# Setup of a fused attention and convolution kernel: the first loads, the second chunk of x, GpSimd's order and VectorE's first factors are placed anew

## The chip, the core and the metric

The kernel runs on one core of a Trainium2 chip. The core has five engines that run side by side: TensorE (PE in the profile, and PEld for its weight loads), VectorE (DVE), ScalarE (ACT), GpSimd (POOL) and SyncE (SP). SP, ACT and POOL can each issue DMAs, and every engine works through its own instructions in the order in which they were written for it. The metric is the time of one execution on the device in microseconds (us), lower is better.

## The reference

Two independent parts, whose outputs are joined along the last axis. Part A is a long convolution of 576 channels over 2048 positions, whose kernel is built from 128 complex exponentials a channel. Part B is attention with 32 query heads of 18 numbers and one shared key and value head.

```
# A: u (1, 2048, 576); A, B, C (576, 128) complex
dt = exp(log_dt)[:, None]
P  = exp((dt * A)[:, :, None] * arange(2048))        # (576, 128, 2048)
K  = einsum("dn,dnl,dn->dl", C, P, dt * B).real      # the convolution's kernel
y  = causal_convolution(u, K) + u * Dskip            # by FFT of length 4096
# B: x (1, 2048, 576), 32 heads, Dh = 18
q = heads(x @ wq);  k = x @ wk;  v = x @ wv          # one k and v for all heads
p = softmax(einsum("bhqd,bkd->bhqk", q, k) * Dh ** -0.5)
b = merge_heads(einsum("bhqk,bkd->bhqd", p, v)) @ wo
out = concatenate([y, b], axis=-1)
```

## The kernel before, in words

**Attention** (class `Attention`) goes over the 2048 queries in four chunks of 512 columns (x0 to x3), in each over 8 groups of four heads, and in each group over 16 blocks of 128 keys. One score tile `s` is 128 keys by two heads by 512 queries: two matmuls (L543), each of the keys `kaug` against one head's queries `aug`. ScalarE turns it into `P` with one exponential (L552 in the first group, L554 later). `product` (L841) multiplies `P` with the values `v_sb` and adds into `ops` (L849). Three score tiles are in flight (`NS = 3`), so the main loop takes three at a time; such a set of three is called a round below. At the end of a group VectorE copies `ops` to `o` (`gather`, L561), and the next group's `ops` can start only then.

The queries of a chunk come from five projections `q` (L437), which VectorE splits in two f16 halves `qh` and `ql`; GpSimd's queue writes them to a DRAM buffer `qd` (L487), and SP's queue fetches each pair of heads back as `aug` (L532). A row `sh` that belongs to every head, a bound on its scores, goes the same way (L523).

**Convolution** (class `Conv`) goes over 12 chunks of 48 channels. `front` makes the kernel of a chunk: `powers` (L1112; ScalarE's Exp and Sin and VectorE's products), `factors` (L1190), `tables` (`tab`, L1256) on VectorE and `kgen` (`kg`, L1287) on TensorE. `back` transforms, multiplies and transforms back (`hu`, `lu`, `hk`, `lk`, `iy` on TensorE, long products on VectorE). These are generators: `Stream.advance` runs one to its next `yield`, and `conv.begin(n)` (L1466) runs the first one n steps, so that its instructions stand at that place in each engine's order.

**What sets the order.** In the main loop a planner (`fill`, L810) keeps a clock `K` with modelled costs (`K.t` for TensorE, `K.v` for VectorE, `K.a` for ScalarE) and puts pieces of the convolution and of the projections between the rounds of scores. All instructions of PE, ACT and DVE stand in source order (L1527); those of POOL are placed by the compiler's scheduler.

**The setup** (`setup`, L234, and the first four rounds of `main`) is where the change lies. It loads `wq[0]` on ScalarE's queue and x0, `wkv` and x1 on SP's; `conv.early()` (L1458) loads the first inputs of the convolution, `dt`, `ab`, `pos` and `raw`, on GpSimd's queue. Then come, in source order:

1. four warm-up products on zeros (`warm`), and `conv.begin(6)`: `powers` to the first Sin;
2. the projection `first` of x0 into keys of chunk 0 and queries of heads 0 to 4 and more (20 matmuls), whose f16 halves `h1` (ScalarE, L292) and `l1` (VectorE, L294) are the first `keys`. Eighteen-row DMAs copy them into `kaug` (L301) and into the first two `aug` (L305), on all three queues;
3. the loads of x2 and x3 on SP's queue (L324, `x_us`, `x_ks` and `x_acc`), and `conv.begin(4)`: the second Sin and the Exp of `powers`;
4. the projection `second` (keys of chunk 1, values of chunks 0 and 1, and queries; 20 matmuls, from x0 and x1), with the bound on the first group's scores between (`small`, `aw_first`, `bias`);
5. `main`: the first round of scores; `keys_1` (L376) splits `second` into halves (`h2`, `l2`), copies them to `kaug` (L355, SP and POOL) and transposes values (`va`); the second round; `keys_23` (L384) projects `third` from x2 and x3 in two pieces around the third round, splits it and copies it to `kaug` in twelve DMAs of SP; `settle` (L396) ends the keys (`vb`, `kmx`, `kmax`) and starts the loads of the other weights and of the convolution's `dft`. After that the planner works.

In the listing `x` is a tile of x0 or x1, and `keys` is the tile that holds all the halves.

## Time and profile before

| | us |
|---|---|
| median of three runs | 1170.29 |
| the three runs | 1166.37 to 1170.54 |
| the profiled execution, its own time | 1168.69 |
| the span of its trace | 1166.9 |
| TensorE busy | 1089.1 |
| VectorE busy | 999.0 |
| ScalarE busy | 998.9 |
| GpSimd busy | 142.1 |

The span runs from the first to the last instruction, 1.8 us less than the execution's own time. Times below count from the span's start. A row of the timeline has start, duration, engine, line, operation, output and inputs, and in brackets how long the engine sat idle before it and what ended that. A row of the chain has start, duration and what the end of the program waited for at that time. A row of the windows has, for each engine, busy time and the number of instructions, and then the granted TensorE clock (PEclk, 1.00 is full), the DMA engines' share and GB/s.

### The profile page before, as it was taken

The page shows a single profiled execution, that of the slowest core. Times are in us where ns is not written, and L with a number is a line of the kernel's source. Part 1 is how long each engine was busy: PE and PEld are TensorE (multiplying, and loading weights), DVE is VectorE, ACT ScalarE, POOL GpSimd, SP SyncE. Part 2 cuts the span into 40 slices and gives each one's busy share as a digit, 9 for nine tenths or more (in the row PEclk, how much of TensorE's full clock was granted, in tenths as well). Part 3 has the DMA queues.
Part 4 walks back from the last instruction along what each step waited for, and adds up shares of the span by engine and source line. Part 5 has one row for each costly group of instructions (what it writes and reads, how often), then busy time and mean ns, then how long its engine had stood idle before and what let it go on. Part 6 is the DMA issues. An engine that isn't in the chain of part 4 may idle for free.

```text
span 1166.9 us, 33114 instructions
## 1 busy us (share of the span) xinstructions
PE 1089.1 (93%) x13898; PEld 393.7 (34%) x13898; DVE 999.0 (86%) x1755; ACT 998.9 (86%) x1052; POOL 142.1 (12%) x258
## 2 busy tenths in 40 slices
PE   7889989999999999899999999989989999999997
PEld 2223333333333333324333333334322333433323
DVE  3668998899899898898899799898798899799693
ACT  4668998889888998998888889888999989899992
POOL 5131221122022000000221100001050000000000
PEclk9899999999999999999999999999999999999999
DMA  7421241213212202022222301202122200311201
GB/s 231 135 57 54 82 159 41 81 33 95 82 58 80 85 28 73 20 87 87 90 77 74 104 22 55 74 28 77 60 83 75 88 29 29 104 47 34 70 29 58
DMA packets 57595, 83.90 MB, mean 72 GB/s; under 512 B 13829, under 2 KB 33867, under 8 KB 56928
## 3 DMA queue, kind: packets, MB, share of 16 engines
q1 hardware_dynamic: 46191, 73.71, 19.1%
q0 software_dynamic: 11024, 7.63, 2.7%
q8 instruction: 111, 1.82, 0.6%
q10 hardware_dynamic: 225, 0.38, 0.1%
q14 instruction: 44, 0.36, 0.1%
HBM read 47.12 MB, written 33.85 MB: 69 GB/s over the span
## 4 chain that ended last, share of the span: by engine, by line
PE 58%; DVE 20%; ACT 11%; issue 6%; DMA 2%; POOL 1%; DVEq 0%; ACTq 0%; SPq 0%; POOLq 0%
PE ops L849 24%; PE s L543 15%; ACT P L554 11%; PE op L194 5%; PE q L437 4%; DVE tab L120 3%; PE iy L194 3%; DVE ks L120 3%; PE kg L1298 3%; DVE acc L120 2%; DVE t L120 2%; PE hu L194 1%; PE hk L194 1%; DVE fr L120 1%; PE fin L194 1%
## 5 line engine op out<-in xcount | busy, mean ns | idle before, releaser
L554 ACT ACTIVATE P<-s 128x1024 f32<-128x1024 f32 x992 | 934.5, 1034 | 119.6 <-PE s L543 117.4
L849 PE MATMUL ops<-P,v_sb 128*32 128x512 f32 x4096 | 510.5, 599 | 10.7 <-DVE o L124 10.4
L543 PE MATMUL s<-aug,kaug 55*128 55x512 f16 x2048 | 308.4, 381 | 42.6 <-ACT P L554 34.8
L543 PEld LDWEIGHTS <-kaug 55*128 55x128 f16 x2048 | 90.6, 94 | 378.0 <-issue 328.8
L849 PEld LDWEIGHTS ops<-P,v_sb 128*32 128x32 f32 x4096 | 117.2, 110 | 168.2 <-issue 127.5
L487 POOL DMA_DIRECT2D qd<-qh x116 | 65.7, 573 | 307.3 <-DVE qh L128 306.9
L437 PE MATMUL q<-x,wq_sb 128*32 128x256 f32 x1360 | 85.2, 386 | 0.2 <-DVE un L136 0.2
L194 PE MATMUL op<-wo_sb,oT 126*32 126x288 f32 (+1 forms) x1080 | 77.2, 410 | 2.6 <-DVE ob L124 1.4
L120 DVE TENSOR_TENSOR tab<-tab,tt 128x576 f32<-128x576 f32 (+1 forms) x72 | 59.1, 820 | 1.4
L124 DVE COPY ksb<-kg 128x192 f32<-128x192 f32 x48 | 17.4, 363 | 49.9 <-PE kg L1298 49.6
L120 DVE TENSOR_TENSOR tab<-tab 128x576 f32<-128x576 f32 (+1 forms) x72 | 58.7, 815 | 0.0
L120 DVE TENSOR_TENSOR tab<-fr,dif 128x576 f32<-128x576 f32 (+1 forms) x72 | 58.7, 815 | 0.0
L120 DVE TENSOR_TENSOR tab<-sum,fr 128x576 f32<-128x576 f32 (+1 forms) x72 | 58.7, 815 | 0.0
L120 DVE TENSOR_TENSOR tt<-fr,sum 128x576 f32<-128x576 f32 (+1 forms) x72 | 58.7, 815 | 0.0
L437 PEld LDWEIGHTS q<-x,wq_sb 128*32 128x32 f32 x1360 | 39.5, 110 | 39.8 <-issue 15.4
L1207 POOL MEMSET fr<- 128x192 f32 x24 | 12.9, 623 | 307.0 <-DVE tt L120 194.6
L120 DVE TENSOR_TENSOR acc<-acc,pt 128x1728 f32<-128x1728 f32 (+2 forms) x36 | 48.6, 1350 | 0.1
L120 DVE TENSOR_TENSOR pt<-us,ks 128x1728 f32<-128x1728 f32 (+2 forms) x36 | 48.3, 1349 | 0.1
L552 ACT ACTIVATE P<-s,bias 128x1024 f32<-128x1024 f32 x32 | 33.2, 1115 | 14.0 <-PE s L543 13.6
L194 PEld LDWEIGHTS op<-wo_sb,oT 126*32 126x32 f32 (+1 forms) x1080 | 30.3, 109 | 43.4 <-issue 17.5
L1298 PEld LDWEIGHTS kg<-tab 128*32 128x32 f32 x2304 | 35.7, 110 | 22.7 <-issue 7.9
L1298 PE MATMUL kg<-tab 128*32 128x64 f32 x2304 | 41.8, 220 | 1.2 <-DVE tab L120 0.8
(177 smaller groups left out, 1023.6 us busy)
## 6 DMA issues: line engine op xcount, KB each, us to landing
od<-o SPq DMA_DIRECT2D x31, 256.0 KB
aug<-qd SPq DMA_DIRECT2D x124, 55.0 KB
u<-u SPq DMA_DIRECT2D x12, 384.0 KB
kd<-ksb SPq DMA_DIRECT2D x12, 384.0 KB
kt<-kd SPq DMA_DIRECT2D x48, 96.0 KB
outa<-u SPq DMA_DIRECT2D x12, 384.0 KB
pw<-pw SPq DMA_DIRECT2D x8, 528.0 KB
oT<-od SPq DMA_DIRECT2D x16, 252.0 KB
```

Of the source, the lines that this page charges most:

```text
L120: return self.v.tensor_tensor(out, *a, **k)
L124: return self.v.tensor_copy(out, *a, **k)
L194: nc.tensor.matmul(ps[j:e], w[:, j:e], x, start=start, stop=stop, tile_position=(0, j))
L437: nc.tensor.matmul(ps[o, 256 * f:256 * f + 256], w[:, k, i], xt[:, k, x], start=(k == 0), stop=(k == 4), tile_position=(0, 32 * j))
L487: q.dma_start(qd[h:h + n, row + d:row + d + nd, cs], src[i1:i1 + n * nd, :cs.stop - cs.start])
L543: nc.tensor.matmul(ps[:, j, :], self.kaug[r, kb * P:(kb + 1) * P], t[r, :], start=True, stop=True)
L552: nc.scalar.activation(pt, ps, AF.Exp, bias=self.bias, scale=SCALE / QQ)
L554: nc.scalar.activation(pt, ps, AF.Exp, scale=SCALE / QQ)
L849: nc.tensor.matmul(o_ps[32 * j:32 * j + 32, :], self.v[:, kb, :], pts[exp(n, j // 2)][:, j % 2, :], start=(kb == 0), stop=(kb == 15), tile ...
L1207: nc.gpsimd.memset(t[:, :, 0:NF:8], one)
L1298: nc.tensor.matmul(ps[32 * g:32 * g + 32, d, :], t[:, :32], t[:, 32:], start=(j == 0), stop=(j == 1), tile_position=(0, 32 * g))
```

## The change

Five things are altered in the setup, and one follows from them.

- The convolution's first `dt`, `ab` and `pos` are issued on ScalarE's queue, behind `wq[0]`, and no longer on GpSimd's. `raw` stays on GpSimd's.
- x1 is loaded after `conv.begin(6)`. A memset by VectorE on a corner of x1 stands ahead of each of its two loads, so SP issues them when VectorE has come to that place.
- Three products on zeros (12 matmuls into `spare`, half a bank of `small`) stand where three fifths of `second` stood. One fifth comes ahead of the bound, one behind it, and the other three after the first round of scores. The bound ends earlier in TensorE's order.
- VectorE makes the first factors inside the setup: `conv.begin(3)` ahead of the first scores, `conv.begin(2)` behind `keys_1` and `conv.begin(1)` ahead of the second piece of `keys_23`. The transposes `va` move behind the second round. The planner's clock gets 3.5 in place of 1.5 there.
- POOL joins the engines in source order.
- The planner starts from another state, so all later pieces are placed anew.

```diff
--- before.py
+++ after.py
@@ -261,8 +261,6 @@
         nc.sync.dma_start(wkv, a["wkv"])
         nc.sync.dma_start(x0[:, 1:3, :], a["xT"][0, :, 1:3, :])
         nc.sync.dma_start(x0[:, 3:5, :], a["xT"][0, :, 3:5, :])
-        nc.sync.dma_start(x1[:, 0:3, :], a["xT"][1, :, 0:3, :])
-        nc.sync.dma_start(x1[:, 3:5, :], a["xT"][1, :, 3:5, :])
         conv.early()
         nc.gpsimd.dma_start(spread[:, 0:140], a["sel"][:, 45:185])
         nc.gpsimd.dma_start(self.sel, a["sel"][:, 0:45])
@@ -284,7 +282,11 @@
         self.todo, self.busy, self.group = [], False, 0
         self.side_work = Stream(self.side(), self.k, 99.0)
         conv.begin(6)
-        p1, small = (self.ps_s.tile([P, 2, CT], F32, tag="s", name=n)[:, 0, :] for n in ("first", "small"))
+        for k0, k1 in ((0, 3), (3, 5)):
+            V.memset(x1[0:1, k0:k1, 0:1], 0.0)
+            nc.sync.dma_start(x1[:, k0:k1, :], a["xT"][1, :, k0:k1, :])
+        p1, small = (self.ps_s.tile([P, 2, CT], F32, tag="s", name=n) for n in ("first", "small"))
+        p1, small, spare = p1[:, 0, :], small[:, 0, :], small[:, 1, 0:256]
         for k in range(5):
             for j in range(3):
                 self.project(p1, j, self.wq[0], 32 * j, 0, k)
@@ -324,17 +326,18 @@
                 nc.sync.dma_start(t[:, :, c - 2, :], a["xT"][c, :, k0:k1, :])
         conv.begin(4)
         self.pa = pa = self.bank(CT, "second")
-        for k in range(3):
-            self.second(k)
+        for _ in range(3):
+            matmul4(nc, spare, self.wo[:, 0, 0:P], self.wo[:, 0, P:P + 256])
         nc.tensor.matmul(small[:, 0:1], spread[:, 0:128], self.km[:, 0:1], start=True, stop=True)
         V.tensor_copy(self.kmax[:, 0:1], small[:, 0:1])
         aw = self.p2.tile([P, P], F32, tag="aw", name="aw_first")
         V.tensor_scalar(aw, ab[:, 0:1].broadcast_to([P, P]), self.kmax[:, 0:1], 1.002, op0=ALU.mult, op1=ALU.mult)
-        for k in range(3, 5):
-            self.second(k)
+        self.second(0)
         matmul4(nc, small[:, 8:12], aw, self.sel[:, 0:4])
         V.tensor_reduce(self.bias, small[:, 8:12], axis=AX.X, op=ALU.max)
         V.tensor_scalar(self.bias, self.bias, -SCALE / QQ, None, op0=ALU.mult)
+        self.second(1)
+        conv.begin(3)
 
     def project(self, ps, j, w, i, c, k):
         self.nc.tensor.matmul(ps[32 * j:32 * j + 32, :], w[:, k, i:i + 32], self.slice(c, k),
@@ -375,14 +378,16 @@
 
     def keys_1(self):
         nc, V = self.nc, self.V
+        for k in range(2, 5):
+            self.second(k)
         h2, l2 = self.parts[2:]
         self.halves(self.pa, h2, l2, 5)
         self.place(1, h2, l2, 0, (nc.sync, nc.gpsimd))
         self.largest(h2, 5)
-        self.values(self.ps_o.tile([P, CT], F32, tag="o", name="va"), 0, slice(1, 3))
 
     def keys_23(self, ks):
         if ks[0] == 0:
+            self.values(self.ps_o.tile([P, CT], F32, tag="o", name="va"), 0, slice(1, 3))
             self.pb = self.bank(CT, "third")
         for k in ks:
             self.third(k)
@@ -880,13 +885,15 @@
             s = self.step
             if r == 0:
                 self.keys_1()
-                K.t += 1.5
+                conv.begin(2)
+                K.t += 3.5
                 continue
             if r == NS:
                 self.keys_23((0, 1))
                 K.t += 2.1
                 continue
             if r == 2 * NS:
+                conv.begin(1)
                 self.keys_23((2, 3, 4))
                 K.t += 2.7
                 continue
@@ -1070,7 +1077,7 @@
         cs = slice(k0 * ND, k1 * ND)
         dt, ab = (self.pf.tile([P, n, 4 * ND], F32, tag=t, name=f"{t}{g}") for n, t in ((1, "dt"), (2, "ab")))
         n = (k1 - k0) * ND
-        q = nc.sync if g else nc.gpsimd
+        q = nc.sync if g else nc.scalar
         q.dma_start(dt[:, 0, :n], self.a["ldt"][cs].partition_broadcast(P))
         q.dma_start(ab[:, :, :n], self.a["pa"][:, :, cs])
         self.next_burst = dt[:, 0, :n], ab[:, :, :n]
@@ -1458,7 +1465,7 @@
     def early(self):
         nc = self.nc
         self.load_burst(0)
-        nc.gpsimd.dma_start(self.pos, self.a["pos"])
+        nc.scalar.dma_start(self.pos, self.a["pos"])
         self.load(0)
         self.n, self.burst = -1, False
         self.streams = [Stream(self.front(0), self.k)]
@@ -1524,7 +1531,7 @@
         at = Attention(tc, ctx, aps, clock)
         cv = Conv(tc, ctx, at.bank, aps, clock)
         cv.at, at.conv = at, cv
-        with tc.manual_schedule(engines={mybir.EngineType.PE, mybir.EngineType.Activation, mybir.EngineType.DVE}):
+        with tc.manual_schedule(engines={mybir.EngineType.PE, mybir.EngineType.Activation, mybir.EngineType.DVE, mybir.EngineType.Pool}):
             cv.setup()
             cv.open(ctx)
             at.open(ctx)
```

At the start, on ScalarE, these are the rows before and after (`dt`, `ab`, `pos` are the convolution's inputs, `pw` its powers, `keys` the halves of the projections):

```order
L259 DMA wq_sb<-wq 128x640
L1135 ACT_TABLE_LOAD
L1135 ACTIVATE dt_139<-dt_139 128x48
L1155 ACT_TABLE_LOAD
L1155 ACTIVATE pw_171<-pw_171 128x528
L292 ACTIVATE keys<-first 128x512
```

```order
L259 DMA wq_sb<-wq 128x640
L1081 DMA dt_137<-ldt 128x48
L1082 DMA ab_138<-pa 128x2x48
L1468 DMA pos_sb<-pos 128x22
L1142 ACT_TABLE_LOAD
L1142 ACTIVATE dt_137<-dt_137 128x48
L1162 ACT_TABLE_LOAD
L1162 ACTIVATE pw_169<-pw_169 128x528
L294 ACTIVATE keys<-first 128x512
```

Three loads moved in ahead of ScalarE's first table load; the Sin of `pw` stands ahead of the halves `keys` in both.

On SP after the change, with the semaphores on which each issue waits (x_126 is x1; DMAHW0 to 7 are eight semaphores that the DMAs of SP and ACT take in turn, each waiting for the one that had it before):

```order
L287 DMA x_126<-xT 128x1536 [waits DMAHW0_49,DVE_49]
L287 DMA x_126<-xT 128x1024 [waits DMAHW1_49,DVE_49]
L303 DMA kaug<-keys 18x512 [waits DMAHW5_49,Activation_49]
L303 DMA kaug<-keys 18x512 [waits DMAHW6_49]
L303 DMA kaug<-keys 18x512 [waits DMAHW7_49,DVE_49]
L303 DMA kaug<-keys 18x512 [waits DMAHW0_49]
L307 DMA aug_114<-keys 18x512 [waits DMAHW1_49]
L307 DMA aug_114<-keys 18x512 [waits DMAHW2_49]
```

The fourth copy to `kaug` now takes DMAHW0 after the first part of x1, and the first copy to `aug_114` takes DMAHW1 after the second part. Before, x1's loads stood ahead of all VectorE work, as the fifth and sixth load of SP.

On VectorE between the bound and the projection of x2 and x3, before (`bias` is the bound, `m` and `pw` are the powers' parts, `fr` and `t` the factors):

```order
L136 TENSOR_REDUCE bias_121<-small 128x1
L128 TENSOR_SCALAR bias_121<-bias_121 128x1
L128 TENSOR_SCALAR keys<-second 128x512
L132 SCALAR_TENSOR_TENSOR keys<-second,keys 128x512
L124 COPY keys<-second 128x512
L136 TENSOR_REDUCE km<-keys 128x1
L128 TENSOR_SCALAR km<-km 128x1
L124 COPY v_sb<-va 128x8x18
L128 TENSOR_SCALAR keys<-third 128x512
```

and after, from the bound to the halves of `second`:

```order
L128 TENSOR_SCALAR bias_121<-bias_121 128x1
L120 TENSOR_TENSOR pw_169<-pw_169,m_170 128x528 x2
L124 COPY fr_274<-pw_169 128x48x4 x2
L124 COPY fr_274<-pw_169 128x48x3
L124 COPY fr_274<-pw_169 128x48x4 x2
L124 COPY fr_274<-pw_169 128x48x3
L128 TENSOR_SCALAR keys<-second 128x512
L132 SCALAR_TENSOR_TENSOR keys<-second,keys 128x512
```

Eight products and copies of the convolution moved in ahead of the halves of `second`; twelve more products `t` and `fr` and seven on `raw` and `w` stand between these and `keys<-third`. Before, all of them stood behind `settle`.

At the end of the first group, on VectorE, before (`qh`, `ql`, `ab`, `aw` belong to the projection q_2, `o` is the copy of the first group's `ops`, `kg` the convolution's kernel from TensorE):

```order
L128 TENSOR_SCALAR qh_2_852<-q_2_741 128x512
L132 SCALAR_TENSOR_TENSOR ql_2_853<-q_2_741,qh_2_852 128x512
L136 TENSOR_REDUCE ab_2_854<-qh_2_852 128x1
L128 TENSOR_SCALAR aw_2_867<-ab_2_854,kmax 128x128
L124 COPY o_0_873<-ops_0_382 128x512
```

and after:

```order
L124 COPY ksb_583<-kg_0_0_788 128x4x16x3
L124 COPY ksb_583<-kg_0_1_837 128x4x16x3
L124 COPY tab_1_863<-fr_274 128x24x2x8 x2
L120 TENSOR_TENSOR tab_1_863<-fr_274,dif_539 128x24x24
L124 COPY o_0_872<-ops_0_439 128x512
```

The copy `o_0` stood behind the four instructions of q_2; it now stands behind the first kernel pieces and three instructions of the next table, and q_2 comes after it.

## The prediction

> **What bounds the kernel now.** I read the page first, then the windows of 50 us, then the chain of waits of the first 120 us, and last the timeline of the setup.
>
> ```profile
> span 1166.9 us, 33114 instructions
> PE 58%; DVE 20%; ACT 11%; issue 6%; DMA 2%; POOL 1%; DVEq 0%; ACTq 0%; SPq 0%; POOLq 0%
> ```
>
> ```profile
> 0.00:50.00 50.00, 40.05 (x286) 11.61 (x287) 20.75 (x70) 24.88 (x26) 21.37 (x43) 0.90 0.53 166
> 50.00:100.00 50.00, 44.36 (x590) 16.31 (x593) 39.51 (x74) 36.92 (x39) 11.46 (x21) 0.97 0.26 82
> 100.00:150.00 50.00, 46.82 (x624) 17.11 (x616) 43.13 (x65) 47.14 (x51) 13.18 (x23) 1.00 0.33 103
> ```
>
> Over the whole span TensorE leads the chain, with VectorE second. From 100 us on TensorE and ScalarE are both busy 94% of the time, so nothing done in the setup makes that stretch shorter. The first 50 us are different: VectorE is busy 20.75 us and ScalarE 24.88, and the clock stands at 0.90. The change works there, and what it saves is a start that comes earlier. The chain tells which waits make the start long:
>
> ```profile
> 2.01 8.57 DMA ab<-pa
> 14.27 0.49 ACT keys L292
> 16.59 2.83 POOL aug L305 x6
> 21.06 5.57 DMA kaug<-keys
> 26.91 3.53 DMA qd<-keys
> 30.91 4.41 PE third L340 x24
> 68.50 1.75 DMA aug<-qd
> ```
>
> First comes a load of 8.57 us for the convolution, which has nothing to do with the first scores except that its Sin stands ahead of the halves `keys` in ScalarE's order. Then come the copies of the first keys and queries, then the copies of the keys of chunk 1, and then the projection of x2 and x3.
>
> **The loads on ScalarE's queue.**
>
> ```profile
> 4.75 0.22 PEld L340 LDWEIGHTS first<-x,wq_sb 128*32 128x32 f32 x6 [0.62 <-DMA wq_sb<-wq]
> 7.50 0.24 ACT L1135 ACTIVATE dt<-dt 128x48 f32<-128x48 f32 x1 [5.02 <-DMA dt<-ldt]
> 10.67 0.26 DVE L120 TENSOR_TENSOR ab<-ab,dt 128x96 f32<-128x96 f32 x1 [8.57 <-DMA ab<-pa]
> 11.96 0.61 PE L340 MATMUL first<-x,wq_sb 128*32 128x512 f32 x3
> 13.63 0.64 ACT L1155 ACTIVATE pw<-pw 128x528 f32<-128x528 f32 x1 [4.59 <-DVE pw L128]
> 14.18 0.58 ACT L292 ACTIVATE keys<-first 128x512 f16<-128x512 f32 x1
> ```
>
> `wq`, 320 KB on ScalarE's queue, had landed by 4.75; `dt`, 24 KB on GpSimd's, by 7.50; `ab`, 48 KB, by 10.67. Behind `wq` the three small loads can be there at 7 at the earliest (`dt`'s own time again, from 4.75 with a share of it), and at 10.67 at the latest if the queue does not matter. I take 9.1, half way between `dt`'s 7.50 and `ab`'s 10.67, because x0's loads are on the DMA engines until about then, whichever queue asks. That gives 1.6 us (ends 0 and 3.7). `first` ends at 11.96 + 0.61 = 12.57, so the halves could start at 12.6, also 1.6 us earlier; x0 has no x1 beside it, so it comes no later. The three issues on ScalarE stand ahead of a table load that waits for nothing, and `dt` comes later than that: nothing.
>
> The Trainium skill speaks against this part. "DMA: Bandwidth & Descriptors", section "Issuing engines are not separate DMA queues", says that all queues run on the same 16 DMA engines and that another issuing engine saves only the time of the issue. By it the 1.6 us would be 0; the gap between `wq` and `ab` above does not decide it, as `wq` was also first in time.
>
> **x1 held back.** SP's issues of x1 now wait for VectorE's last `pw` product, which ends where the Sin starts: 13.6 - 1.6 = 12.0. The nearest row for such a load is `x_us`, two loads of 512 KB:
>
> ```profile
> 19.65 0.92 SPq L324 DMA_DIRECT2D x_us<-xT  x2
> 24.86 0.19 PEld L340 LDWEIGHTS third<-x_us,wkv_sb 128*32 128x32 f32 x6 [0.87 <-DMA x_us<-xT]
> 14.79 3.28 SPq L301 DMA_DIRECT2D kaug<-keys  x4
> 18.11 1.44 SPq L305 DMA_DIRECT2D aug<-keys  x2
> 20.36 6.13 ACT L552 ACTIVATE P<-s,bias 128x1024 f32<-128x1024 f32 x6
> 30.44 0.16 PEld L543 LDWEIGHTS <-kaug 55*128 55x128 f16 x2 [2.33 <-DMA kaug<-keys]
> ```
>
> They took 5.2 us for 1 MB, so x1's 1.25 MB, asked for at 12.0, is there in parts at about 16.3 and 17.5. SP's fourth copy to `kaug` takes over the semaphore of the first part, the next copy that of the second. SP's copies cost 0.82 us each: x1's own two issues to 13.4, three copies to 15.9, the fourth at 16.3, then the two of `aug` from 17.5 (0.72 each) to 18.9. So `x_us` is asked for at 18.9 and not at 19.65: of the 1.6 us only 0.75 are left on SP. The copies of chunk 1's keys are held up behind the x2 and x3 data (the 30.44 row), so they move by the same 0.75. Bounds: with the loads at 7, 3.5 us; with the loads at 10.67, x1 arrives 1.6 us later and this is -0.85. A first `P` about 0.9 us earlier than 20.36 hangs on the same.
>
> **`second` behind the first scores, and the products on zeros.** TensorE does the same 20 matmuls. The 12 on zeros lie in the wait for x1 between about 11 and 16.3 us: nothing, as long as x1 comes after 13. What matters is the clock:
>
> ```profile
> 20.70:24.10 3.40, 1.99 (x13) 0.86 (x14) 1.53 (x4) 3.40 (x4) 3.40 (x8) 1.00 0.95 316
> 24.10:27.50 3.40, 3.40 (x16) 0.75 (x12) 0.00 (x0) 2.39 (x3) 1.56 (x4) 0.50 1.05 366
> 31.00:34.30 3.30, 3.30 (x20) 0.73 (x19) 0.00 (x0) 1.06 (x1) 0.00 (x0) 0.50 0.01 1
> 41.40:44.30 2.90, 2.90 (x18) 0.49 (x14) 2.87 (x14) 1.24 (x2) 1.25 (x1) 0.50 0.10 25
> 71.90:75.30 3.40, 3.40 (x28) 1.06 (x20) 1.97 (x3) 1.72 (x2) 0.00 (x0) 0.50 0.04 11
> ```
>
> Four stretches of 3.4 us run at half clock, each behind one in which TensorE was busy for some 2 us of 3.4. Half a clock costs 1.7 us where TensorE is what is waited for. Three fifths of `second` are as many matmuls as the 4.41 us of `third` in the chain, of which 3.3 ran at half clock: 3.3 / 2 + 1.1, or 2.7 us at full clock. They now fill the stretch ahead of 24.1. I count one of the two stretches on `third` as gone with chance a half: 0.9 us.
>
> **Factors in VectorE's gap.**
>
> ```profile
> 35.39 0.69 DVE L128 TENSOR_SCALAR keys<-third 128x512 f16<-128x512 f32 x1 [13.12 <-PE third L340]
> 41.60 1.32 DVE L120 TENSOR_TENSOR pw<-pw,m 128x528 f32<-128x528 f32 x2
> 42.96 1.14 DVE L124 COPY fr<-pw 128x192 f32<-128x192 f32 x6
> 43.05 1.83 POOL L1207 MEMSET fr<- 128x192 f32 x2 [12.36 <-DVE pw L120]
> 43.90:46.40 2.50, 2.32 (x8) 0.87 0.17 39
> 48.30:52.00 3.70, 3.60 (x8) 1.00 0.99 355
> 51.80:53.20 1.40, 1.26 (x10) 1.00 0.93 380
> ```
>
> The moved products are the three stretches, 2.32 + 3.60 + 1.26 = 7.2 us, and 1.32 + 1.14 = 2.5 us of `pw` and `fr` ahead of the halves of `second`. The gap was 13.12 us. But the halves of `second` come some 3 us later than before (22.5: scores at about 19.5, then the 2.7 us that moved), and their own four passes (2.8 us at the 0.69 of `keys<-third`) plus 7.2 plus the copy `v_sb` end at about 33, while `third` would end at 33 to 34.5. So VectorE comes just in time; cover gone, it costs up to 1 us. `settle` thus starts 0.75 + 0.9 = 1.65 us earlier, say 1.7 (ends -1.9 and 4.4). GpSimd's source order puts its memsets of `fr`, 1.8 us, ahead of the copies of chunk 1's keys; these are issued at 22.5 and wait for the data of x2 and x3 anyway: nothing.
>
> **What a fuller VectorE gives back at 60 to 82 us.**
>
> ```profile
> 70.29 0.80 PE L543 MATMUL s<-aug,kaug 55*128 55x512 f16 x5 [1.76 <-DMA aug<-qd]
> 80.32 1.07 PE L849 MATMUL ops<-P,v_sb 128*32 128x512 f32 x8 [2.19 <-DVE o L124]
> 79.58 0.68 DVE L124 COPY o<-ops 128x512 f32<-128x512 f32 x1
> ```
>
> Three losses stand here: 1.76 us for the queries of the second group (projection q_1, VectorE's halves, GpSimd's stores, a fetch); 1.7 us of half clock from 71.9, behind that wait; and 2.19 us because the copy `o` stood behind the halves of q_2 on VectorE. After the change q_1 starts one round earlier, and VectorE has 9.7 us of products behind it: I take half of the first (0.9) and, as the half clock follows from the wait, half of the second (0.9). `o` no longer waits for q_2; two kernel pieces and three table operations stand ahead, in a round that is long enough: 1.9 of 2.19.
>
> **The rest.** The convolution now runs three to four rounds ahead of its old place to the end. TensorE's and ScalarE's work is the same, so I count 0, between the ends of the `o` waits below.
>
> Sum: 1.7 + 0.9 + 0.9 + 1.9 = 5.4 us. The profiled execution took 1168.69, with 1.8 us around its span; 1168.7 - 5.4 = 1163.3, so 1163. That execution is 1.6 us under the median of 1170.29, against which it reads 0.6% less. Under about 0.5% (5.9 us) a run of this kernel cannot be told from no change.
>
> **Rivals.**
>
> *The loads land no earlier.* The small loads then share the engines with x0's 1.3 MB as they did before, and `ab` is there at 10.67 again. Then the setup gives -0.85 + 0.9, about 0, and the later stretch perhaps 2: 1167. For it speaks that `wq`, the fast load on that queue, had the engines nearly to itself; against it that x1's 1.25 MB are gone from the engines. The skill's rule quoted above would give this case.
>
> *VectorE is late for `third`.* If the halves of `second` start at 24 and not 22.5, the products end at 34.5 and push `keys<-third`, the last keys and all weights with it. The start then gains nothing, only the rounds behind it do: 1166.
>
> *The clock stays up.* If all of the half-clock stretches at 24, 31, 41 and 72 go, that is 4 x 1.7 = 6.8 us, of which 1.8 are in my sum: 1158. The Trainium skill, "TensorE: Matmul & The Clock Gate", Part 1, ties half clock to an idle window of about 3.4 us; the row 20.70 shows 1.99 us of work in the window and half clock after it, so the trace does not bear out that a window must be idle. That keeps this case small.
>
> *The copies `o` wait more (the other side).* Each of 31 groups ends with a copy `o` that stands in VectorE's order wherever the planner put it.
>
> ```profile
> PE ops L849 <- DVE o L124: 10.4, 11, 2.6
> ```
>
> Eleven waits cost 10.4 us, 0.95 on average. All later places are new. If 16 more copies fall behind table products, that is 15 us: 1178. It turns the sign from 6 more on (5.4 us), and shows as slower from about 14. Against it: as many places may get better as worse, and the planner does the same as before.
>
> **Chances.** Forecast (1157 to 1166): 0.43. Loads no earlier: 0.17. VectorE late: 0.14. Clock up: 0.12. Copies `o`: 0.14. Faster by over 0.5% means under 1164.4: two thirds of the forecast (0.29), nearly all of the clock case (0.12) and a little of the others (0.03), 0.44. Slower means over 1176: most of the `o` case, 0.12. The same: 0.44. The range goes from 1156, below which lies half of the clock case (0.06), to 1173, above which lies the `o` case.
>
> **What would show it.** The first `ab` product at 9.1 and not 10.67; x1's landing on SP's wait at 16.3; the first `P` near 19.5; `keys<-third` near 33.7 with TensorE, not VectorE, as releaser; no wait of `ops` for the first `o`. I am wrong if x1 lands after 19 and `x_us` is asked for later than 19.65, if VectorE's products end after `third`, or if `ops` waits for `o` for more than 16 us in all.

## The result and the profile after

| | before | after |
|---|---|---|
| median of 12 runs, us | 1169.58 | 1170.26 |
| lowest and highest | 1166.37 to 1174.05 | 1168.10 to 1171.41 |
| the profiled execution, its own time | 1168.69 | 1168.61 |
| its span | 1166.9 | 1166.8 |

The ratio of after to before is 1.0002, with a 95% interval from 0.9989 to 1.0015: the change makes no difference that can be measured. The forecast of 1163.0 was 7 us too low.

The page of the changed kernel (its span, and the shares of the chain that ended last) and its windows of 50 us:

```profile
span 1166.8 us, 33185 instructions
PE 56%; DVE 23%; ACT 11%; issue 6%; DMA 3%; POOL 1%; ACTq 0%; DVEq 0%; SPq 0%
```

```profile
0.00:50.00 50.00, 37.75 (x314) 11.70 (x318) 28.97 (x92) 24.06 (x25) 19.15 (x40) 0.93 0.52 164
50.00:100.00 50.00, 46.96 (x690) 18.13 (x686) 40.26 (x63) 43.91 (x47) 11.40 (x20) 1.00 0.33 103
100.00:150.00 50.00, 42.96 (x506) 14.71 (x500) 46.35 (x87) 46.15 (x46) 14.87 (x26) 1.00 0.35 113
```

Between 50 and 100 us ScalarE does 7.0 us more work than before and the clock stands at 1.00 and not at 0.97. TensorE's account of the whole span shows where that went. It was busy 1085.5 us against 1089.1, in part since less of its work ran at half clock (mean granted clock 0.993 against 0.991), and so idle 81.3 us against 77.8. Up to 100 us it idled 15.3 us (100 less 37.75 and 46.96), before the change 15.6. From 100 us on it had 3.9 us less to do than before (busy 1000.8 us against 1004.7), about what the first 100 us had won, and there it idled 66.0 us against 62.2: 3.8 us are given back.

The chain of waits of the first 45 us, and the timeline of the setup:

```profile
2.40 9.02 DMA pos_sb<-pos
13.96 4.22 DMA x<-xT
18.19 4.49 DMA kaug<-keys
23.58 2.76 PE second L343 x24
28.69 4.30 DMA kaug<-keys
33.63 2.71 PE third L343 x24
```

```profile
10.71 0.26 DVE L120 TENSOR_TENSOR ab<-ab,dt 128x96 f32<-128x96 f32 x1 [8.61 <-DMA ab<-pa]
11.52 0.71 DVE L120 TENSOR_TENSOR pw<-ab,pos_sb 128x528 f32<-128x528 f32 x1 [0.33 <-DMA pos_sb<-pos]
13.94 0.64 ACT L1162 ACTIVATE pw<-pw 128x528 f32<-128x528 f32 x1 [4.93 <-DVE x L143]
13.96 0.80 SPq L287 DMA_DIRECT2D x<-xT  x2
14.49 0.58 ACT L294 ACTIVATE keys<-first 128x512 f16<-128x512 f32 x1
15.09 3.81 SPq L303 DMA_DIRECT2D kaug<-keys  x4
18.31 1.05 PE L343 MATMUL second<-x,wkv_sb 128*32 128x512 f32 x3 [1.05 <-DMA x<-xT]
19.75 1.44 SPq L307 DMA_DIRECT2D aug<-keys  x2
21.29 1.16 SPq L326 DMA_DIRECT2D x_us<-xT  x2
23.19 1.11 ACT L557 ACTIVATE P<-s,bias 128x1024 f32<-128x1024 f32 x1 [2.48 <-PE s L548]
26.36 0.69 DVE L128 TENSOR_SCALAR keys<-second 128x512 f16<-128x512 f32 x1 [3.12 <-PE second L343]
29.02 1.92 PE L343 MATMUL third<-x_us,wkv_sb 128*32 128x512 f32 x16
33.56 1.92 PE L343 MATMUL third<-x_ks,wkv_sb 128*32 128x512 f32 x16
35.31 1.04 PE L343 MATMUL third<-x_acc,wkv_sb 128*32 128x512 f32 x8
36.47 0.68 DVE L128 TENSOR_SCALAR keys<-third 128x512 f16<-128x512 f32 x1
40.67 1.24 PE L412 MATMUL kmx<-km,spread_sb 128*128 128x4 f32 x12 [1.13 <-DVE km L128]
```

`ab` is there at 10.71, where it was at 10.67. The chain still begins with a small load for the convolution, now `pos`, which landed at 11.42. x1 is asked for at 13.96; its first part lands 4.2 us later, and `second` starts on it at 18.31. SP's fourth copy to `kaug` and the copies of `aug` stand behind x1, so `x_us` is asked for at 21.29 and not at 19.65, and the first `P` comes at 23.19 and not at 20.36. `third` then wins most of it back: its three rows take 4.9 us, all at full clock, against 8.9 before, where they were:

```profile
23.85 4.21 PE L340 MATMUL third<-x_us,wkv_sb 128*32 128x512 f32 x16
30.84 3.62 PE L340 MATMUL third<-x_ks,wkv_sb 128*32 128x512 f32 x16
34.23 1.09 PE L340 MATMUL third<-x_acc,wkv_sb 128*32 128x512 f32 x8
```

`kmx`, the product of `settle` that follows the last keys, was at 39.65 and is at 40.67.

The windows of the stretches at half clock, and one ahead of the first of them:

```profile
15.80:18.30 2.50, 0.38 (x2) 0.32 (x3) 2.04 (x9) 0.28 (x1) 2.50 (x6) 1.00 0.94 368
18.30:21.70 3.40, 3.39 (x24) 0.83 (x24) 1.27 (x4) 2.38 (x3) 1.59 (x4) 0.51 0.49 166
41.60:45.00 3.40, 3.40 (x23) 0.85 (x27) 2.97 (x17) 1.01 (x2) 0.00 (x0) 0.60 0.11 24
71.90:75.30 3.40, 3.40 (x54) 1.59 (x50) 3.40 (x6) 3.40 (x5) 0.00 (x0) 1.00 0.21 77
253.70:257.10 3.40, 3.26 (x15) 0.49 (x16) 3.40 (x6) 0.69 (x1) 1.77 (x4) 0.53 0.50 151
```

Of the four that the prediction quoted, those at 24, 31 and 72 are gone and the one at 42 is there. A new one at 18.3 lies on `second`, behind the wait for x1, and another at 253.7. One near 851 is there before and after.

What is given back shows in the waits of TensorE from 95 us on (engine, line, releaser: us in total, times, longest), first of the kernel before, then of the changed one:

```profile
PE s L543 <- ACT P L554: 34.8, 95, 0.5
PE ops L849 <- DVE o L124: 8.2, 10, 2.6
PE iy L194 <- DVE ql L132: 3.1, 2, 2.6
```

```profile
PE s L548 <- ACT P L559: 36.6, 92, 1.0
PE ops L854 <- DVE o L124: 13.0, 14, 2.4
PE hu L194 <- DVE scu L120: 2.6, 3, 1.6
```

`ops` waits 4.8 us longer for the copies `o`, `s` 1.8 us longer for `P`; the wait of `iy`, 3.1 us, is gone. The longest wait for `o` ends at 253.7. VectorE's timeline there:

```profile
249.53 0.68 DVE L128 TENSOR_SCALAR qh<-q 128x512 f16<-128x512 f32 x1
250.25 0.69 DVE L132 SCALAR_TENSOR_TENSOR ql<-q,qh 128x512 f16<-128x512 f32 x1
250.85 0.68 DVE L136 TENSOR_REDUCE ab<-qh 128x1 f32<-128x512 f16 x1
251.56 0.29 DVE L128 TENSOR_SCALAR aw<-ab,kmax 128x128 f32<-128x128 f32 x1
251.77 0.75 DVE L120 TENSOR_TENSOR tab<-fr,dif 128x576 f32<-128x576 f32 x1
252.44 0.75 DVE L120 TENSOR_TENSOR pt<-us,ks 128x576 f32<-128x576 f32 x1
253.10 0.68 DVE L124 COPY o<-ops 128x512 f32<-128x512 f32 x1
```

The group's products were done, but the halves of a query projection and two pieces of the convolution stood ahead of `o`. The convolution is further ahead now, so at each group's end other work stands there. At this end, the sixth group's, the wait is 2.38 us, and 1.56 before; at the third, eighth and ninth group's 1.19, 1.34 and 0.88, and 0, 0.38 and 0.17 before. Some places got better: at the fourth's the wait is 0, and 0.67 before, and the longest one before, 2.63 us at the 21st, is 0.18 now. The sum is what got worse.

### The profile page after: what moved, and what is told of

Read it like the earlier page. It is cut to its first block, busy times and chain, and to the rows that moved or that the text cites. A ratio compares the mean times of both kernels' runs of the same rounds, so it can differ in the third digit from the quotient of the medians.

```text
span 1166.8 us, 33185 instructions
## 1 busy us (share of the span) xinstructions
PE 1085.5 (93%) x13922; PEld 393.2 (34%) x13922; DVE 1000.5 (86%) x1762; ACT 999.8 (86%) x1052; POOL 140.8 (12%) x255
## 4 chain that ended last, share of the span: by engine, by line
PE 56%; DVE 23%; ACT 11%; issue 6%; DMA 3%; POOL 1%; ACTq 0%; DVEq 0%; SPq 0%
PE ops L854 23%; PE s L548 15%; ACT P L559 10%; DVE tab L120 4%; PE op L194 4%; PE q L442 4%; DVE ks L120 3%; PE iy L194 3%; PE kg L1305 3%; DVE acc L120 3%; DVE pt L120 2%; DVE t L120 2%; PE lu L194 1%; PE hk L194 1%; PE hu L194 1%
## 5 line engine op out<-in xcount | busy, mean ns | idle before, releaser
L559 ACT ACTIVATE P<-s 128x1024 f32<-128x1024 f32 x992 | 935.2, 1033 | 120.8 <-PE s L548 119.5
L854 PE MATMUL ops<-P,v_sb 128*32 128x512 f32 x4096 | 509.2, 597 | 13.2 <-DVE o L124 13.0
L194 PE MATMUL op<-wo_sb,oT 126*32 126x288 f32 (+1 forms) x1120 | 80.4, 410 | 1.6 <-DVE ob L124 1.0
L557 ACT ACTIVATE P<-s,bias 128x1024 f32<-128x1024 f32 x32 | 33.3, 1116 | 13.6 <-PE s L548 13.3
```

Source lines behind the costliest of these rows:

```text
L194: nc.tensor.matmul(ps[j:e], w[:, j:e], x, start=start, stop=stop, tile_position=(0, j))
L557: nc.scalar.activation(pt, ps, AF.Exp, bias=self.bias, scale=SCALE / QQ)
L559: nc.scalar.activation(pt, ps, AF.Exp, scale=SCALE / QQ)
L854: nc.tensor.matmul(o_ps[32 * j:32 * j + 32, :], self.v[:, kb, :], pts[exp(n, j // 2)][:, j % 2, :], start=(kb == 0), stop=(kb == 15), tile ...
```

## The experiments

Below, "order" is that of TensorE, VectorE and ScalarE from the main loop on. In the first four runs there are two: the order before, and that of the changed kernel, which comes with the three calls that make factors in VectorE's gap. GpSimd stands in source order wherever the setup is "after", and is placed by the compiler in all other runs; no run tests that part of the change alone. "kmx" is the start of `kmx` in the profiled execution, "`o` waits" those of `ops` from 95 us on. Ratios are to the kernel before on the same chip.

One execution was profiled of each kernel, and `kmx` differs between executions of one setup: 40.67, 42.88 and 41.90 in `after`, e5 and e14, 40.19, 38.50, 38.22 and 38.53 in e3, e7, e12 and e13. A good part of this is the projection `first`, of which some matmuls run at half clock in part of the executions (1.06 us each and not 0.6): it ended at 13.1 us in `after`, but at 14.7 and 14.8 in e5 and e14, and at 15.8 in e3, against 12.6 in the kernel before.

| run | setup | order | median us | ratio (95%) | kmx | `o` waits |
|---|---|---|---|---|---|---|
| before | before | before | 1169.58 | | 39.65 | 8.2 |
| after | after | after | 1170.26 | 1.0002 (0.9989 to 1.0015) | 40.67 | 13.0 |
| e1 | after, x1 early | after | 1169.18 | 0.9999 (0.9986 to 1.0012) | 40.16 | 11.8 |
| e2 | after, no factors in the gap | before | 1170.32 | 1.0005 (0.9991 to 1.0019) | 41.68 | 8.1 |
| e3 | before, factors in the gap | after | 1166.80 | 0.9991 (0.9974 to 1.0008) | 40.19 | 13.3 |
| e4 | after, GpSimd's queue | after | 1169.68 | 0.9999 (0.9986 to 1.0012) | 40.42 | 11.7 |
| e5 | after | rule 0.3 | 1159.84 | 0.9913 (0.9896 to 0.9930) | 42.88 | 7.5 |
| e6 | before | rule 0 on the order before | 1183.52 | 1.0121 (1.0101 to 1.0142) | 39.57 | 8.1 |
| e7 | as e3 | rule 0.3 | 1157.44 | 0.9900 (0.9884 to 0.9916) | 38.50 | 7.5 |
| e8 | as e3, keys ahead of Sin | rule 0.3 | 1157.33 | 0.9893 (0.9876 to 0.9911) | 40.14 | 7.4 |
| e9 | as e3, x1 held back | rule 0.3 | 1161.36 | 0.9938 (0.9925 to 0.9951) | 42.28 | 7.6 |
| e10 | as e3, `second` in two parts, no products on zeros | rule 0.3 | 1159.78 | 0.9926 (0.9912 to 0.9939) | 40.80 | 7.7 |
| e11 | as e3, ScalarE's queue | rule 0.3 | 1160.07 | 0.9926 (0.9914 to 0.9939) | 40.74 | 7.7 |
| e12 | as e3 | rule 0 | 1163.54 | 0.9959 (0.9943 to 0.9975) | 38.22 | 8.0 |
| e13 | as e7, beside e14 | rule 0.3 | 1159.09 | 0.9914 (0.9900 to 0.9927) | 38.53 | 7.5 |
| e14 | as e5, beside e13 | rule 0.3 | 1159.79 | 0.9921 (0.9907 to 0.9934) | 41.90 | 7.5 |
| e15 | after, GpSimd's queue | rule 0.3 | 1159.20 | 0.9919 (0.9905 to 0.9934) | 39.77 | 7.5 |

### Setup and order, each with the other's partner

**e1**, x1 loaded early in the changed kernel:

```
+        nc.sync.dma_start(x1[:, 0:3, :], a["xT"][1, :, 0:3, :])
+        nc.sync.dma_start(x1[:, 3:5, :], a["xT"][1, :, 3:5, :])
...
-        for k0, k1 in ((0, 3), (3, 5)):
-            V.memset(x1[0:1, k0:k1, 0:1], 0.0)
-            nc.sync.dma_start(x1[:, k0:k1, :], a["xT"][1, :, k0:k1, :])
```

> The changed kernel with x1's two loads asked for behind x0's again; the 12 products on zeros, the later `second`, the queues and the order from the main loop on are those of the changed kernel. Theory 'start': the first `P` at 23.19 instead of 20.36 comes from x1's landing at 18.3 alone and reaches the end; here `second` starts near 15, `x_us` is asked for near 19.7, the first `P` comes at 20 to 21, and the time is 2 to 3 us under the changed kernel's 1170.3, about 1168. Theory 'slack': what is won in the first 100 us is absorbed later whatever the order; then the first `P` comes at 20 to 21 too, and the time stays at 1170 within 1 us. Theory 'clock': the late x1 keeps TensorE idle until 18.3 and it is that which gives `third` its full clock; then `third` is at half clock here, settle is no earlier, and the time is 1170 to 1172.

The first `P` came at 22.59, not at 20 to 21, so 'start' falls: with the small loads on ScalarE's queue, x1 early comes with a later `pos`. The timeline of e1:

```profile
13.32 0.71 DVE L120 TENSOR_TENSOR pw<-ab,pos_sb 128x528 f32<-128x528 f32 x1 [1.21 <-DMA pos_sb<-pos]
16.30 0.58 ACT L293 ACTIVATE keys<-first 128x512 f16<-128x512 f32 x1
```

`pos` was waited for until 13.32 (11.52 with x1 held back) and the keys came at 16.30. `third` kept its full clock, against 'clock', and the time is within 1.1 us of the changed kernel's. Its two long rows took 1.92 to 1.93 us in all seven profiles of the changed setup and its variants (`after`, e1, e2, e4, e5, e14 and e15), so its full clock is not the luck of one execution.

**e2**, the changed kernel without the factors in the gap:

```
-        conv.begin(3)
...
-                conv.begin(2)
-                K.t += 3.5
+                K.t += 1.5
...
-                conv.begin(1)
```

> The changed kernel without the three calls that make factors in VectorE's gap (and with the planner's 1.5 us): x1 held back, bound ahead, queues and GpSimd's order as changed; from the main loop on, the order of all engines is that of the kernel before. Theory 'start and order': the hold-back costs about 1 us where the main loop is entered, the lead of 6 us won between 74 and 95 us is missing, and so is what the new order gave back later; `ops` waits for `o` about 10.4 us in all as before, and the time is 1170 to 1172. Theory 'gap gain is real': without the factors the time is 4 us or more above the changed kernel's, 1174 or more.

1170.32 with 8.1 us of `o` waits: as 'start and order' says. The order before brings back its own shorter waits, whatever the setup.

**e3**, the factors alone in the kernel before:

```
+        conv.begin(3)
...
-                K.t += 1.5
+                conv.begin(2)
+                K.t += 3.5
...
+                conv.begin(1)
```

> The kernel before with only the factors made in VectorE's gap (three calls added, the planner's 3.5 us): x1 early, all of `second` ahead of the bound, small loads on GpSimd's queue; from the main loop on, the order is that of the changed kernel. Theory 'start': x1's hold-back hides a gain of the factors; here the first `P` is at 20.4 as before, 4 to 6 us are won between 70 and 95 us, about as much is given back by longer waits of `ops` for `o` (13 us in all and not 10.4), and the time is 1167 to 1169. Theory 'slack': 1169.5 to 1170.5, no different from before. If VectorE's factors come in the way of the first keys, the time is over 1171.

1166.80, near 'start', and 13.3 us of `o` waits with the setup before: these waits belong to the order and not to the setup. The first `P` came at 22.02 and not at 20.4, behind the late `first` of this execution. The interval of the ratio reaches over 1, so the gain of 2.2 us is not shown.

**e4**, the small loads back on GpSimd's queue:

```
-        q = nc.sync if g else nc.scalar
+        q = nc.sync if g else nc.gpsimd
...
-        nc.scalar.dma_start(self.pos, self.a["pos"])
+        nc.gpsimd.dma_start(self.pos, self.a["pos"])
```

> The changed kernel with the convolution's three small loads on GpSimd's queue again; all else as changed. Theory 'shared engines': the first product on `ab` starts at 10.5 to 10.8 as in both kernels, whichever queue asks, and the time is 1170.3 within 0.7 us. Theory 'queue': GpSimd's issues stand in source order now, so the loads come 0.5 to 1 us later than on ScalarE's queue, x1 with them, and the time is 0.5 to 1.5 us more.

The time does not tell the theories apart, but `ab` was there at 10.17, earlier than either had it and than with ScalarE's queue. Over all profiles the first product on `ab` starts at 9.83 to 10.67 with GpSimd's queue (11 executions) and at 10.71 to 11.63 with ScalarE's (six).

The product on `pos` shows the queue and the hold-back together. With GpSimd's queue it starts at 10.8 to 11.2 with x1 early (eight executions) and at 10.4 to 10.9 with x1 held back (three). With ScalarE's queue it starts at 13.2 and 13.3 with x1 early (e11, e1) and at 11.5 to 12.0 with x1 held back (four). So the move to ScalarE's queue made `pos` late, and the hold-back of x1 repaired a part of that.

### Another order with the same work

A rule was put into the planner: while the 14th and 15th key blocks of a group are put in, VectorE's other work may not be planned further ahead than a limit, 0.3 us in **e5** (on the changed kernel) and **e7** (on e3), 0 in **e6** (on the kernel before).

```
-        if self.kind == "v" and (k.t < self.ready or k.v > k.t + self.ahead):
+        if self.kind == "v" and (k.t < self.ready or k.v > k.t + (min(self.ahead, 0.3) if k.near else self.ahead)):
...
+            K.near = 13 <= kb < 15
```

> The changed kernel with one rule added to the planner: while the 14th and 15th key blocks of a group are put in, VectorE's other work may run ahead of TensorE by 0.3 us and not 0.7 or more, so that less of it stands ahead of the copy `o`. The setup is the changed kernel's, the order from the main loop on a new one. Theory 'o waits': what the factors won at 60 to 100 us is given back because `ops` waits for `o` 13.2 us after 95 us, against 8.5 before the change; with the rule these waits fall to 3 to 6 us, and the time by about as much, to 1161 to 1165. Theory 'slack': the waits fall as well, but TensorE then waits elsewhere (for `P`, or in `q`, `op`, `hu`), since three engines are near their limit in turn; the time stays at 1168 to 1171.

> The kernel before with the same rule (ahead by 0 us there), which has 8.5 us of such waits after 95 us. Theory 'o waits': they fall to 3 to 5 us and the time by 3 to 5 us, to 1164 to 1166. Theory 'slack': no change, 1168 to 1171.

> The kernel before with the factors in VectorE's gap (as in the third run) and the rule of 0.3 us; from the main loop on, its order is that of the changed kernel with the rule. Theory 'o waits': 1160 to 1164, and within 1.5 us of the changed kernel with the rule, as the setups differ by no more than executions do. Theory 'slack': 1166 to 1169.

e5 took 1159.84 and e7 1157.44. Both are under the ranges of 'o waits' (1161 to 1165 and 1160 to 1164), and e7 is 2.4 us under e5 and not within 1.5; 'slack' falls in both. What is won in the setup can be kept to the end, if the order behind it does not lose it. `o` is only part of it: the waits of `ops` fell by 5.5 us, to 7.5 and not to 3 to 6, and the time by 10.4.

```profile
PE ops L856 <- DVE o L125: 7.5, 10, 2.4
```

That is e5. ScalarE's wait for scores fell too, in the page of e5 to 108.1 us from the changed kernel's 119.5, and TensorE's idle time in all fell from 81.3 us to 73.0. e6 fits neither theory. Its `o` waits stayed at 8.1 us, and the time rose by 14 us. Most of that is one other wait, which its waits of TensorE from 95 us on show:

```profile
PE iy L195 <- DVE w L121: 10.0, 1, 10.0
PE ops L851 <- DVE o L125: 8.1, 10, 1.4
```

The one wait of 10.0 us lies behind the last scores. There VectorE finished the last chunk of the convolution alone, from 1147 to 1157 us. That the rule had kept this work back until nothing stood beside it is the likely reason; no run tests it.

**e8** moves one step of e7, the halves of `first` ahead of the Sin:

```
-        conv.begin(6)
+        conv.begin(5)
...
         nc.scalar.activation(h1, p1, AF.Copy, scale=QS)
+        conv.begin(1)
```

> The kernel of the run before this one with one step moved: ScalarE makes the halves `keys` of `first` ahead of the convolution's Sin instead of behind it; VectorE's and TensorE's order is the same. Theory 'start': the keys come 0.6 to 1.6 us earlier wherever `first` ends before the Sin does, and with them the first `P`, `x_us` and the end: 0.5 to 1.5 us less than the run before. Theory 'slack': no difference, since `first` itself often ends later than the Sin could start (at half clock, or with x0 late).

1157.33, no difference. In its profiled execution `first` itself ended at 15.3, at half clock.

**e12** is e7 with a limit of 0:

```
-        if self.kind == "v" and (k.t < self.ready or k.v > k.t + (min(self.ahead, 0.3) if k.near else self.ahead)):
+        if self.kind == "v" and (k.t < self.ready or k.v > k.t + (min(self.ahead, 0.0) if k.near else self.ahead)):
```

> The seventh run's kernel with 0 us in the rule instead of 0.3: the same setup and the same rule, another order from the first group on. By the planner's own clock, `o` is behind TensorE by 12.8 us in all, against 6.5 with 0.3 us and 21.3 without the rule. Theory 'o waits': the waits of `ops` for `o` after 95 us are 9 to 11 us, between the 7.7 with 0.3 and the 13.6 without the rule, and the time is 1160 to 1164, between those kernels' 1157.4 and 1166.8. Theory 'any order': the time goes by where all waits happen to fall, and not by `o` alone: it can lie anywhere from 1155 to 1170 with the waits for `o` in that range.

8.0 us of `o` waits, below the range of 9 to 11, and yet 1163.54, 6 us more than e7 with 7.5. So the waits for `o` alone do not give the time, and 'any order' is nearer. TensorE's idle time in all points the same way, 77.9 us against 75.9 and 73.1 in two executions of e7's kernel (e7 and e13), but does not give the whole difference.

### The parts of the setup, one at a time

e9, e10 and e11 put three parts of the change's setup into e7, one each. **e9**, x1 held back:

```
-        nc.sync.dma_start(x1[:, 0:3, :], a["xT"][1, :, 0:3, :])
-        nc.sync.dma_start(x1[:, 3:5, :], a["xT"][1, :, 3:5, :])
...
         conv.begin(6)
+        for k0, k1 in ((0, 3), (3, 5)):
+            V.memset(x1[0:1, k0:k1, 0:1], 0.0)
+            nc.sync.dma_start(x1[:, k0:k1, :], a["xT"][1, :, k0:k1, :])
```

**e10**, `second` in two parts (`va` moves to `keys_23` with it). The 12 products on zeros, which the change has in place of the first three fifths and which the expectation names, are not in this kernel:

```
-        for k in range(3):
-            self.second(k)
...
-        for k in range(3, 5):
-            self.second(k)
+        self.second(0)
...
+        self.second(1)
...
+        for k in range(2, 5):
+            self.second(k)
         h2, l2 = self.parts[2:]
```

**e11**, the small loads on ScalarE's queue:

```
-        q = nc.sync if g else nc.gpsimd
+        q = nc.sync if g else nc.scalar
...
-        nc.gpsimd.dma_start(self.pos, self.a["pos"])
+        nc.scalar.dma_start(self.pos, self.a["pos"])
```

> The seventh run's kernel (the setup before with the factors in VectorE's gap, and the rule; 1157.4 us) with x1's two loads held back behind VectorE's last product ahead of the Sin, as in the changed kernel. The changed kernel's setup in the same order took 1159.8, 2.4 us more; this run and the next two put one part of it in each. Theory 'hold-back': it is x1; `second` then starts at 18 and not at 15.6, `x_us` is asked for 1.6 us later, and the time is 1159 to 1160. Theory 'shared DMA engines': x0 and the small loads come as much earlier as x1 comes later, and the time is 1157.4 within 0.8 us.

> The seventh run's kernel with `second` in two parts, the products on zeros in its place, and `va` made ahead of `third`, as in the changed kernel; x1 early, small loads on GpSimd's queue. Theory 'spread': the halves of `second` come near 25 instead of 20.5, the keys of chunk 1 and the factors after them, and the time is 1159 to 1160. Theory 'filled wait': the later halves lie in the wait for the data of x2 and x3, TensorE is busy ahead of `third` and `third` keeps its full clock, and the time is 1156.5 to 1158.

> The seventh run's kernel with the three small loads on ScalarE's queue. Over the profiles so far the first product on `ab` started at 10.2 to 10.7 with the loads on GpSimd's queue and at 10.7 to 11.6 with them on ScalarE's, and x0's middle part was there at 8.8 to 10.4 and at 9.3. Theory 'queue order': `ab` later by 0.8 us, with it the Sin and the keys, and the time is 1158 to 1159. Theory 'shared DMA engines': what `ab` loses x0 wins, and the time is 1157.4 within 0.6 us.

Each alone came out slower than e7: 3.9, 2.3 and 2.6 us. That is the direction of 'hold-back', 'spread' and 'queue order', with e9 and e11 over their ranges. In e10 TensorE waited 2.9 us for copies of the keys ahead of the second piece of `third`, which then ran at half clock (3.35 us), against 'filled wait'. e9 shows why the hold-back and the bound belong together. Its timeline:

```profile
17.14 1.07 PE L343 MATMUL second<-x,wkv_sb 128*32 128x512 f32 x3 [4.56 <-DMA x<-xT]
25.19 0.15 DVE L129 TENSOR_SCALAR bias<-bias 128x1 f32<-128x1 f32 x1
25.45 2.12 ACT L555 ACTIVATE P<-s,bias 128x1024 f32<-128x1024 f32 x2 [5.88 <-PE s L546]
```

The bound stands behind all of `second`, which waits for x1 and then runs at half clock, and the first `P` is at 25.45. e11 has the fault of e1: x1 early on SP's queue with the small loads on ScalarE's, and `pos` waited for until 13.21.

Since e7 and these three stood on different chips, e7 and e5 were run again beside each other, as **e13** and **e14**, with **e15**, which is e14 with the small loads on GpSimd's queue.

> The seventh run's kernel (the setup before with the factors alone, rule of 0.3 us) beside the next two. Theory 'setup costs': 1157 to 1158, 2 us or more under the next run. Theory 'no difference': within 0.8 us of the next run.

> The fifth run's kernel (the changed kernel's setup, rule of 0.3 us). Theory 'setup costs': 1159.5 to 1160.5. Theory 'no difference': within 0.8 us of the run before, at 1158 to 1159.

> The fifth run's kernel with the small loads on GpSimd's queue: x1 held back and `second` in two parts with the bound ahead of three of them. Theory 'cover': the hold-back alone cost 3.9 us because the bound stood behind all of `second` (25.25 us instead of 18.8); with `second` in two parts the bound comes near 21 again and the two together cost 1.5 to 2.5 us, 1159 to 1160. Theory 'sum': 3.9 and 2.3 us add up, 1163 or more.

Side by side the difference of the setups is 0.7 us in the medians, 'no difference', and e15 lies between: 'cover', not 'sum'. In the profiled executions `kmx` was at 38.53, 41.90 and 39.77. So the changed setup entered the main loop 3.4 us later than the factors alone here. How much of this is the queue's is open: e14 and e15 are 2.1 us apart, but `first` ended at 14.8 in e14 and at 12.8 in e15, and between `after` and e4, the same two setups in another order, it is 0.25 us, with `first` at 13.1 and 16.7. What reaches the end lies between 0.7 us (here) and 2.4 us (e5 against e7). No run shows a gain from it. What the single parts cost is not settled, as e7's kernel came out 1.7 us higher the second time; only the interval of e9 lies clear of that of e7, and it overlaps that of e13. Nor do the parts add up: 8.8 us one at a time, 0.7 to 2.4 together.

## Why the prediction was wrong

**The loads on ScalarE's queue: the first step that failed.** `ab` was to be there at 9.1 and was at 10.71; from this the Sin, the halves, x1 and `x_us` all slid by about two us. The step took "half way" from the row of `wq`, which was also first in time, as the text itself noted. The first rival had this case. The rule quoted from the Trainium skill, "DMA: Bandwidth & Descriptors", section "Issuing engines are not separate DMA queues", gave 0 us and was right that nothing is won; e4 and the other profiles go further, with `ab` up to 1 us later on ScalarE's queue.

**x1 held back.** The mechanism was right and its sizes too: asked for at 13.96, x1 was there 4.3 us later (16.3 less 12.0 was forecast), and SP's copies waited for it. The row that the forecast cites, 5.2 us for 1 MB, gives 3.9 and 6.5 us for the two parts by proportion; how it came to 4.3 and 5.5 it does not say. With the late start `x_us` came 1.64 us later instead of 0.75 earlier. The lower bound of -0.85 was passed by 0.8 us: `pos` came later still, so that x1 was asked for 0.35 us later than in that case, and its second part took 0.3 us longer, to 19.75. The upper bound of 3.5 does not follow from its own terms: loads at 7 and not at 9.1 add 2.1 to 0.75, which is 2.85.

**`second` and the clock.** Mis-sized. Half of one stretch, 0.9 us, was counted; both on `third` went, and its rows shrank by 4.0 us, while one new stretch fell on `second`. This is the cause that the clock rival named, for three of its four stretches. `kmx` is 1.0 us later all the same: the setup's term of +1.7 measured -1.0, and this execution was a mild one, as `kmx` came 2.3 to 3.2 us later than before in e14 and e5.

**Factors in VectorE's gap.** Right in kind. The halves of `second` came at 26.36 and not at 22.5, and VectorE's products still ended just as `third` did: `keys<-third` starts 0.1 us behind `third` (35.31 + 1.04), without a wait: VectorE, and not TensorE, came last, by that much.

**What a fuller VectorE gives back at 60 to 82 us.** Right: the stretch at 71.9 stands at clock 1.00, `ops` does not wait for the first `o`, and the query wait of 1.76 us is 0.65:

```profile
69.57 0.80 PE L548 MATMUL s<-aug,kaug 55*128 55x512 f16 x5 [0.65 <-DMA aug<-qd]
72.73 0.69 DVE L124 COPY o<-ops 128x512 f32<-128x512 f32 x1
```

**The rest: the second step that failed, and the larger one.** It was counted as 0, because TensorE's and ScalarE's work is the same; TensorE idles 3.8 us more from 100 us on, and `ops` waits 4.8 us more for `o`. The 94% for both engines, with which the prediction opened, is the row of 100 to 150 us alone: from 100 us to the end ScalarE was busy 937.1 of 1066.9 us, 88%. The same work with less waiting fits into less time, as e5 shows. These waits come again in e1, e3 and e4 (11.7 to 13.3 us) and are 8.1 in e2, so they belong to the new order. The rival with the `o` copies named the mechanism but only as 15 us or nothing. Its 15 us by its chance of 0.14, some 2 us, belonged in the sum. Its sign of being wrong, over 16 us of such waits, was not reached (13.0); that of x1 was (its second part there at 19.75, `x_us` asked for at 21.29). Of the 5.4 us, then, by the account of these two executions, 2.7 are missing in the setup and 3.8 in the rest; 4.8 and not 3.7 were won at 60 to 100 us (the 3.8 of the first 100 us and the 1.0 lost in the setup), which leaves 0.

That a new order can cost or win more than the whole change is shown by the same work in other orders: 1157.4, 1163.5 and 1166.8 us (e7, e12, e3) with one setup. Why e5's order is 10.4 us better than the changed kernel's, with the same setup, is shown for 5.5 us, the `o` waits; for the rest only that other waits shrank. What GpSimd's source order does by itself is open.

## What to carry to other kernels

Where an order comes from a planner, a change that shifts work by a few rounds gives every later wait a new place: forecast that as a term with a size, from the waits that such places have cost, and not as 0. Before a load is moved to another queue, see what else is on the DMA engines at that time: here `ab` and `pos` came later on the new queue in every profile, most of all with the big load x1 asked for early, and holding x1 back repaired only a part. Here the order was worth more than the setup: a limit on how far the work ahead of a group's last copy may run made the kernel 0.9 to 1.0% faster (ratio 0.9900, 0.9884 to 0.9916; again 0.9914, 0.9900 to 0.9927). It is no rule to carry over: with another limit on the order before it made the kernel 1.2% slower (e6). Each order has to be measured. And one profile of a kernel does not give its setup to better than 2 us or so, when a projection in it runs at half clock in some executions only.

## What the hardware showed

The stretches at half clock come and go between executions of the same order. The window from 253.5 us of the changed kernel, behind the 2.4 us wait for `o`, and the same window of e3, behind the same wait:

```profile
253.50:257.00 3.50, 3.16 (x14) 0.48 (x14) 3.50 (x6) 0.59 (x1) 1.97 (x4) 0.56 0.49 147
```

```profile
253.50:257.00 3.50, 2.90 (x26) 0.79 (x30) 3.50 (x5) 1.41 (x2) 2.23 (x5) 1.00 0.49 148
```

By estimate one such stretch costs 1.5 us where TensorE is waited for (half of some 3 us). The executions of e3 lie between 1164.53 and 1172.72 us, the first with a mean granted clock of 0.995, the last with 0.986.

In the changed kernel three of the stretches follow one with TensorE nearly idle: 0.38 us of work in 2.5 ahead of 18.30, 0.46 in 2.7 ahead of 253.70, 0.64 in 2.8 ahead of 850.80. That is nearer to the rule of the Trainium skill, "TensorE: Matmul & The Clock Gate", Part 1, of an idle window, than the row of 20.70 to 24.10 in the prediction, with 1.99 us of work, which remains an exception to it. It is not the only one: the 3.4 us ahead of the stretches at 31, 41 and 72 of the kernel before hold 1.56, 2.27 and 1.64 us of work.
